# Three blocks of one expert moved ahead of the block table, beside the last scatters

## The chip, the cores and the metric

The kernel runs on one core of a Trainium2 chip, as one program in one launch. Its time is the device time of that launch in microseconds (us), the median of several runs. The work is written out in program order for each engine: PE (matrix products), DVE (vector), ACT (activations), POOL (GpSimd), and SP, which issues most of the DMAs. An engine carries out its own list in order and waits for the others by semaphores. [...]

## The reference

```python
X = np.fft.fft(np.fft.fft(x, axis=1), axis=2).real          # x: 8 x 3072 x 256
t = X.reshape(24576, 256)
logits = t @ w_gate                                          # 8 experts
e = np.argmax(logits, axis=1); gate = softmax(logits)[e]
y[e == k] = gate * (np.maximum(t @ w1[k], 0) @ w2[k])        # w1: 256 x 1024, w2: 1024 x 256
h = y @ w_in                                                 # 256 x 2048, w_in and w_out in float64
g = (a0 + a1 h + a2 h^2 + a3 h^3) / (1 + |b0||h| + |b1| h^2 + 1e-6)
out = g @ w_out                                              # 2048 x 256
```

## The kernel before, in words

**Phase 1** computes the Fourier transform, gate and sorting in 16 steps (`NS`), two for each of the 8 batch rows. A step has four first products (`stage1`, L438, PSUM pool psA), three groups of second products (`second`, L459 and L461), whose result y goes to SBUF through ACT and DVE (L465, L468; seven buffers), the squared norms on ACT (L496), the gate on DVE (`gate_a`, from L477), ranks within the expert on PE (`gate_rank`, L504 to L509, PSUM pool psS with one buffer), and positions, running counts `run` and gate values on DVE (`gate_b`, L519 to L537). Then POOL scatters 128 token rows at a time with an indirect DMA (L549) into `xs` in HBM, which has a region of R = 24832 rows for each expert. A row holds 256 numbers, the token's number and its gate. The gate of step s is finished in step s + 2 (`finish`), that of the last two steps in parts.

Beside that, each step takes one of 16 jobs: a weight matrix of one expert (`w1` or `w2`) is loaded, its norm summed (`job_sum`, L594, a product with a column of ones into `pa`, also in psS), scaled by a power of two, split into two f16 parts and stored in `ws` in HBM.

**The tail** (L834 to L931) follows the sixteenth step: the rest of the gate, the last twelve scatters, zero rows behind the last token of every expert (`c_z`, L855, each address a register that SP reads from `runi`), the block table on DVE (L865 to L931), and `partition_all_reduce` on POOL (L916) for the row scale `sx`. The table gives for each of the 103 blocks (`NSB`) of 256 rows the expert's weight rows (`widx`), the row in `xs` and the place in `ys` (`offi`), and a factor `rj`.

**Start-up.** A block j of an expert is four pieces: `m1a(j, 0)` and `m1a(j, 1)` (24 matmuls each, then hhi on ACT, L1136, and hlo on DVE, L1137) and `m1b(j, 0)` and `m1b(j, 1)` (24 each, then yw on ACT and DVE, the store to `ys`, and the token numbers to `idd`). Before it, `load(j)` brings its rows (`xr`, L1070), `pairs` splits them into f16 halves (xp; L1091 on ACT and L1092 on DVE for the first two blocks, POOL behind that), `transp` turns them on PE (L1105) and DVE copies them (xt, L1106). Weights come to `wslot[j % 2]`, for the first two blocks by SP (`gather_first`, L1320), then by POOL (`gather`, L908). The first 36 pieces (blocks 0 to 8, `np_`) run with nothing but a generator beside them: `prologue`, which decodes the float64 words of `w_in` and `w_out` quarter by quarter on DVE (`decode`, L207 to L215), splits them and ends with the scalar `og` (L1063). It has 33 steps; the loop calls one after each piece but i = 30, and the rest at i = 32.

**Unit loop.** Then come 385 units of the rational part (`m2a` and so on; the first activation is at L1231) with one piece beside each unit, until the blocks are used up. Block j goes to `ys` for good, and unit groups read `ys` in order, eight blocks behind.

The lists' order is the order of the code; no planner moves anything. Of the code that the steps below touch, the loop of the start-up and the zero rows:

```python
ins_z = [nc.sync.dma_start(out=xs[E * R:E * R + TB, :], in_=cst["c_z"])]
for e in range(E):
    v = nc.sync.value_load(runi[0:1, e:e + 1], min_val=e * R, max_val=e * R + NT)
    ins_z.append(nc.sync.dma_start(out=xs[ds(v, TB), :], in_=cst["c_z"]))
...
for i in range(np_):
    if i == 4 * LAG:
        step(100)
        bound_rows(0)
    piece(i, True)
    if i != 4 * LAG - 2:
        step(1)
```

Of the kernel before, what the change touches and what calls it, by code (L numbers as in the profile page):

```python
# [20 lines left out]
P = 128  # L21
# [8 lines left out]
DX = D + 2  # L30
R = 8 * S + TB
# [97 lines left out]
def fourier_moe_rational_kernel(ctx, tc, xl, wg, w1, w2, w_in, w_out, av, bv, cst, out):  # L129
# [48 lines left out]

    def pow2floor(dst, src):
# [9 lines left out]
    mq_in = keep.tile([P, 4], F32, name="mq_in")  # L189
    TINY = float(np.array([897 << 20], np.int32).view(np.float32)[0])  # L190
# [12 lines left out]
    def decode(r, dst, mx):  # L203
# [11 lines left out]
        V.tensor_reduce(out=mx, in_=dst, axis=AX.X, op=ALU.max, apply_absolute_value=True)  # L215

# [3 lines left out]
    with ExitStack() as c1:  # L220
# [24 lines left out]
        rc, onesf = carve(0, 137), carve(0, P)  # L245
        rs = cp.tile([P, 2, 137], F32, name="rs")
        fb = carve(0, 64).rearrange("p (i s b) -> p i s b", i=4, s=2)
        ids = carve(0, 24).rearrange("p (h t) -> p h t", h=2)
        msk, bigm = carve(0, 13), carve(0, 13)
        upto = carve(0, E * E).rearrange("p (a b) -> p a b", b=E)  # L250
# [340 lines left out]
        def job_sum(n):  # L591

            pa = psS.tile([P, 512], F32, tag="ss", name="pa")
# [87 lines left out]

        def edge_prep():
# [28 lines left out]
        nc.sync.dma_start(out=upto.rearrange("p a b -> p (a b)"), in_=cst["c_up"])  # L711
# [4 lines left out]
        for s in range(NS + 1):  # L716
# [4 lines left out]
            if on:  # L721
# [4 lines left out]
                if s > 1:  # L726
                    column_row(b, jh, u)
                stage1(b, jh, eo, 0, u)
# [88 lines left out]
            if s == NS - 1:  # L817
                gate_rank((p, 1), 4)
# [16 lines left out]
        p = NS - 1  # L835
        for q in range(2):
            load_words(q, raw_in[q])
# [3 lines left out]
        part_gate(p, 1)  # L841
        gate_rank((p, 1), 4)
# [3 lines left out]
        top_norm(*nq)  # L846
        *last, nq = part(p, 1)
        top_norm(*nq)
        V.tensor_copy(out=runi, in_=run)

# [8 lines left out]

        nbi = keep.tile([P, E], I32, name="nbi")
        nb = keep.tile([P, E], F32, name="nb")
        ctok = keep.tile([P, E], F32, name="ctok")
        V.tensor_tensor(out=nbi, in0=run, in1=ebase, op=ALU.subtract)  # L865
        V.tensor_scalar(out=nbi, in0=nbi, scalar1=8, scalar2=None, op0=ALU.logical_shift_right)
        V.tensor_copy(out=nb, in_=nbi)
# [564 lines left out]
```

## Time and profile before

| | us |
|---|---|
| median of 3 runs | 3607.03 (3605.4 to 3608.28) |
| profiled execution, device time | 3599.72 |
| its span, first to last instruction | 3597.9 |
| PE busy | 3460.9 (96%) |
| ACT busy | 3182.4 (88%) |
| DVE busy | 3049.6 (85%) |
| POOL busy | 2952.4 (82%) |
| mean granted clock of PE | 0.985 |

Times in the rows are microseconds from the start of the span, of one execution. A busy time is the sum over an engine's instructions; matmuls are pipelined, so theirs overlap a little. In brackets behind a row stands how long the engine was idle before it and what ended that. `SPq` and `POOLq` are the queues of SP and POOL themselves (issuing, waiting, reading registers). L12 is line 12 of the kernel.

### The profile page before, as it was taken

To read this page: it belongs to the slowest core of one execution; us is meant where nothing else is said; L and a number is where in the kernel's file an instruction comes from. 1 tells how busy PE (TensorE), PEld (TensorE's weight loads), DVE (VectorE), ACT (ScalarE), POOL (GpSimd) and SP (SyncE) were. 2 spreads that over 40 slices of the span, in tenths; PEclk is the share of its full clock that TensorE was granted. 3 is DMA by queue.
4 is the path that set the end of the run, shared out by engine and by line. 5 is a ranking of instruction groups with operands and counts; after the bars stand their busy time and mean duration, and the time that the engine had idled before them with its cause. 6 is when DMAs were issued, how large, how long until landed. Compare 5 with 4: busy or idle time off the path is not lost.

```text
span 3597.9 us, 75912 instructions
## 1 busy us (share of the span) xinstructions
PE 3460.9 (96%) x29948; PEld 2992.3 (83%) x29948; DVE 3049.6 (85%) x3483; ACT 3182.4 (88%) x4117; POOL 2952.4 (82%) x2840
## 2 busy tenths in 40 slices
PE   7998489999999999999999999999999999999997
PEld 4665378888888888888888888888888888888886
DVE  7886678888888888888888888888888888888887
ACT  5777349999999999999999999999999999999997
POOL 1666458888888888888888888888888888888887
PEclk9999699999999999999999999999999999999999
DMA  7675543321151112411151115121331113311110
GB/s 295 242 250 192 187 93 60 69 45 39 45 87 44 44 45 47 83 41 45 43 91 39 44 42 89 45 42 42 67 66 42 46 44 67 63 43 42 45 34 19
DMA packets 343974, 270.39 MB, mean 75 GB/s; under 512 B 181406, under 2 KB 318758, under 8 KB 336304
## 3 DMA queue, kind: packets, MB, share of 16 engines
q1 hardware_dynamic: 310528, 185.57, 20.7%
q0 software_dynamic: 33088, 79.97, 9.0%
q8 instruction: 234, 3.83, 0.6%
q14 instruction: 124, 1.02, 0.1%
HBM read 329.27 MB, written 96.92 MB: 118 GB/s over the span
## 4 chain that ended last, share of the span: by engine, by line
POOL 39%; ACT 29%; issue 14%; PE 7%; DVE 6%; DMA 3%; another core or an unknown queue 1%; SPq 0%; POOLq 0%; DVEq 0%; ACTq 0%
POOL glo L1265 12%; POOL bnd L1188 5%; POOL out_dram L1290 5%; ACT ghi L1264 5%; ACT hhi L1136 5%; POOL wslot L908 3%; ACT h L1249 3%; ACT L L1247 3%; POOL xr L1087 2%; PE po L1277 2%; PE h L1116 1%; PE h L1119 1%; PE h L1117 1%; POOL xp L1088 1%; DMA xs<-y,sli 1%
## 5 line engine op out<-in xcount | busy, mean ns | idle before, releaser
L1116 PE MATMUL h<-yr,win 128*128 128x256 f16 x3072 | 754.0, 273 | 3.1 <-DVE u__48174 L1252 1.7
L1117 PE MATMUL h<-yr,win 128*128 128x256 f16 x3072 | 753.9, 273 | 0.0
L1277 PE MATMUL po<-wout,ghi 128*128 128x256 f16 x6144 | 734.5, 273 | 8.5 <-POOL ghi L1262 7.0
L1277 PEld LDWEIGHTS <-ghi 128*128 128x128 f16 x6144 | 601.0, 98 | 80.2 <-POOL ghi L1262 8.3
L1119 PE MATMUL h<-yr,win 128*128 128x256 f16 x3072 | 586.4, 273 | 0.0
L1249 ACT ACTIVATE h<-L,bnd 128x1024 f32<-128x1024 f32 x385 | 429.7, 1116 | 35.9 <-DVE u__48728 L1240 0.7
L1116 PE MATMUL h<-xt,wslot 128*128 128x256 f16 x1648 | 405.8, 273 | 13.7 <-DVE hlo L1137 7.0
L1117 PE MATMUL h<-xt,wslot 128*128 128x256 f16 x1648 | 405.9, 273 | 0.0
L1277 PE MATMUL po<-wout,glo 128*128 128x256 f16 x3072 | 399.2, 273 | 1.4 <-POOL glo L1265 1.4
L1117 PEld LDWEIGHTS <-wslot 128*128 128x128 f16 x3296 | 323.1, 98 | 68.0 <-issue 31.5
L1116 PE MATMUL py<-hhi,wslot 128*128 128x256 f16 x1648 | 373.7, 274 | 4.3 <-ACT hhi L1136 2.9
L1117 PE MATMUL py<-hhi,wslot 128*128 128x256 f16 x1648 | 373.6, 274 | 0.0
L1116 PEld LDWEIGHTS <-wslot 128*128 128x128 f16 x3296 | 323.4, 98 | 47.4 <-issue 5.2
L1119 PEld LDWEIGHTS <-wslot 128*128 128x128 f16 x3296 | 323.8, 98 | 42.9 <-issue 4.3
L549 POOL DMA_INDIRECT xs<-y,sli x192 | 209.1, 1089 | 166.5 <-ACT sq L496 97.3
L1277 PEld LDWEIGHTS <-glo 128*128 128x128 bf16 x3072 | 300.4, 98 | 38.0 <-POOL glo L1265 3.1
L1116 PEld LDWEIGHTS <-win 128*128 128x128 f16 x3072 | 300.6, 98 | 36.6 <-DVE u__48174 L1252 1.9
L1117 PEld LDWEIGHTS <-win 128*128 128x128 f16 x3072 | 300.6, 98 | 36.6 <-issue 1.8
L1119 PEld LDWEIGHTS <-win 128*128 128x128 f16 x3072 | 300.6, 98 | 34.8
L1119 PE MATMUL h<-xt,wslot 128*128 128x256 f16 x1648 | 315.9, 273 | 0.0
L1137 DVE SCALAR_TENSOR_TENSOR hlo<-h,hhi 128x1024 f16<-128x1024 f32 x206 | 250.8, 1218 | 8.2 <-ACT hhi L1136 8.2
L1290 POOL DMA_INDIRECT out_dram<-o,id x192 | 199.2, 1038 | 49.5 <-issue 43.8
(4904 smaller groups left out, 9381.3 us busy)
## 6 DMA issues: line engine op xcount, KB each, us to landing
xr<-xs SPq DMA_DIRECT2D x103, 258.0 KB
ys<-yw SPq DMA_DIRECT2D x103, 256.0 KB
yr<-ys SPq DMA_DIRECT2D x96, 256.0 KB
xh<-x_l SPq DMA_DIRECT2D x14, 1536.0 KB
wf<-in_moe_w_dram SPq DMA_DIRECT2D x16, 1024.0 KB
ws<-wh SPq DMA_DIRECT2D x16, 1024.0 KB
wslot<-ws SPq DMA_DIRECT2D x4, 1024.0 KB
xh<-x_l SPq DMA_DIRECT2D x4, 768.0 KB
```

Of the source, the lines that this page charges most:

```text
L549: ins = nc.gpsimd.indirect_dma_start(out=xs, out_offset=bass.IndirectOffsetOnAxis(ap=sli[:, t0 + t:t0 + t + 1], axis=0), in_=y[:, t], in_o ...
L1116: nc.tensor.matmul(ps, lhsT=wa[i], rhs=xa[i], start=i == 0, stop=False)
L1117: nc.tensor.matmul(ps, lhsT=wb[i], rhs=xa[i], start=False, stop=False)
L1119: nc.tensor.matmul(ps, lhsT=wa[i], rhs=xb[i], start=False, stop=i == n - 1)
L1136: nc.scalar.activation(out=hhi[:, sl], in_=ps, func=AF.Relu)
L1137: V.scalar_tensor_tensor(out=hlo[:, sl], in0=ps, scalar=0.0, in1=hhi[:, sl], op0=ALU.max, op1=ALU.subtract)
L1188: nc.gpsimd.tensor_scalar(out=out, in0=in0, scalar1=a, scalar2=b, op0=op0, op1=op1)
L1249: nc.scalar.activation(out=ps, in_=L, func=AF.Exp, scale=-1.0, bias=st["bnd", j][3])
L1264: nc.scalar.activation(out=ghi, in_=w_, func=AF.Copy)
L1265: (V if fs[0] else nc.gpsimd).tensor_tensor(out=glo, in0=w_, in1=ghi, op=ALU.subtract)
L1277: nc.tensor.matmul(ps[:, q], lhsT=g[:, f - fs[0], q * P:(q + 1) * P], rhs=wout[:, h, 4 * u + f], start=g is ghi and u == 0 and f == 0 and ...
L1290: ins = nc.gpsimd.indirect_dma_start(out=out, out_offset=bass.IndirectOffsetOnAxis(ap=t[:, q:q + 1], axis=0), in_=o[:, q], in_offset=None, ...
```

## The change

At s = 14, when the tokens of steps 0 to 12 have been counted and their scatters are queued on POOL, the new `fullest` picks the expert that has most rows so far, on DVE, and has POOL reduce the largest norm until then over the partitions. In the last step, `early_rows` loads the first three blocks (K = 3, 768 rows) of that expert from `xs`, and `early_weights` its two weight halves to `wslot[0]`. `early_scale` gives them a row scale `sxe` of their own. In the tail these blocks 0 to 2 are computed: pairs, transposes, m1a and m1b stand between the operations of the gate, the scatters and the block table, which becomes a generator in two parts. What m1b gives is only copied from PSUM to `yf`; it is scaled by `ex1` and stored (`rows_out`) in the start-up. The table counts three blocks fewer for that expert and starts its places behind them. SP now issues the weight loads of block 3 ahead of the zero rows, the loads of blocks 3 to 5 behind them. The start-up loop runs from piece 12 to 35, with two prologue steps at i = 15, 18, 21, 24 and 27; `bound_rows(0)` comes ahead of the remaining steps. `pa` of `job_sum` moves from psS to psA. Constants that lay in `wslot[0]` get tiles of their own, because early weights now go there; `upto` is loaded later. `np_` and the unit loop stay as they are.

```diff
+K = 3
...
+        def fullest():
+            cnt, best = [gp.tile([P, E], F32, tag="cnt", name="cnt") for _ in range(2)]
+            V.tensor_tensor(out=cnt, in0=run, in1=ebase, op=ALU.subtract)
+            V.tensor_reduce(out=ex1, in_=cnt, axis=AX.X, op=ALU.max)
...
+            V.tensor_reduce(out=ex1, in_=nrm, axis=AX.X, op=ALU.max)
+            nc.gpsimd.partition_all_reduce(ex2, ex1, P, bass.bass_isa.ReduceOp.max)
+        def early_rows():
+            v = nc.sync.value_load(epos[0:1, 0:1], min_val=0, max_val=(E - 1) * R)
+            for k in range(K):
+                t = xe[k]
+                nc.sync.dma_start(out=t, in_=xs[ds(v + k * TB, TB), :].rearrange("(t p) c -> p t c", p=P))
...
+        def early_weights(h):
+            v = nc.sync.value_load(epos[0:1, 1:2], min_val=0, max_val=(E - 1) * P)
+            c = slice(4096 * h, 4096 * h + 4096)
+            nc.sync.dma_start(out=wslot[0][:, c], in_=ws[ds(v, P), c])
...
         def job_sum(n):
-            pa = psS.tile([P, 512], F32, tag="ss", name="pa")
+            pa = psA.tile([P, 512], F32, tag="s1", name="pa")
...
+                if s == NS - 1:
+                    early_rows()
                 stage1(b, jh, eo, 0, u)
...
                 send(*finish(s - 2))
+                if s == NS - 2:
+                    fullest()
             for n in old:
                 job_rest(n, 3)
                 job_store(n)
+            if s == NS - 1:
+                early_weights(0)
...
             if s == NS - 1:
+                early_weights(1)
+                early_scale()
...
+        for k in range(K):
+            st["x", k] = xe[k]
+            nc.sync.dma_start(out=idd[k * TB:(k + 1) * TB, :].rearrange("(t p) c -> p (t c)", p=P),
+                              in_=xe[k][:, :, D].bitcast(I32))
         for q in range(2):
-            load_words(q, raw_in[q])
+            pairs(0, q)
+        transp(0)
+        m1a(0, 0, True)
         gate_rank((p, 0), 8)
         second_norm(p, 2)
         ys_, sli, nq = part(p, 0)
         part_gate(p, 1)
+        m1a(0, 1, True)
         gate_rank((p, 1), 4)
         scatter(ys_[0], sli, 0)
         scatter(ys_[1][:, 0:2], sli, 4)
         rest = ys_[1][:, 2:4], sli, 6
         top_norm(*nq)
+        for q in range(2):
+            pairs(1, q)
+        m1b(0, 0, True)
+        transp(1)
         *last, nq = part(p, 1)
         top_norm(*nq)
         V.tensor_copy(out=runi, in_=run)
+        scatter(*rest)
+        send(*last)
+        V.tensor_reduce(out=nx1, in_=nrm, axis=AX.X, op=ALU.max)
+        nc.gpsimd.partition_all_reduce(nx2, nx1, P, bass.bass_isa.ReduceOp.max)
+        m1b(0, 1, True)
+        table = block_table()
+        m1a(1, 0, True)
+        for q in range(2):
+            pairs(2, q)
+        m1a(1, 1, True)
+        transp(2)
+        next(table)
+        for h in range(2):
+            gather_first(K, h)
         ins_z = [nc.sync.dma_start(out=xs[E * R:E * R + TB, :], in_=cst["c_z"])]
...
+        m1b(1, 0, True)
+        m1b(1, 1, True)
+        m1a(2, 0, True)
+        m1a(2, 1, True)
+        next(table)
+        m1b(2, 0, True)
+        m1b(2, 1, True)
...
+    load(K)
+    load(K + 1)
+    load(K + 2)
...
+    row_scale()
+    for q in range(2):
+        pairs(K, q)
...
-    for i in range(np_):
+    for i in range(4 * K, np_):
...
         if i == 4 * LAG:
+            bound_rows(0)
             step(100)
-            bound_rows(0)
         piece(i, True)
+        if i < 5 * K:
+            k = (i - 4 * K - 1) % K
+            rows_out(k, yf[k], ex1)
+            if k == K - 1:
+                load_words(1, raw_in[1])
         if i != 4 * LAG - 2:
-            step(1)
+            step(2 if i > 4 * K and i % 3 == 0 else 1)
```

In the diff, blank lines within functions are left out. Inside the early blocks, `pairs` uses ACT and DVE, `m1a` takes its PSUM from psB, `m1b` and the transposes from psA.

## Rows read from the trace of the kernel before

**Rows 1.** The page: span and instructions.

```profile
span 3597.9 us, 75912 instructions
```

**Rows 2.** Busy time by stretches; columns: us long, busy per engine, clock, DMA.

```profile
390.00:400.00 10.00, 0.38 (x8) 0.29 (x8) 7.40 (x39) 1.84 (x8) 5.12 (x6) 0.50 0.24 79
...
429.26:532.54 103.28, 91.82 (x850) 80.91 (x848) 86.49 (x115) 45.74 (x60) 54.82 (x62) 0.98 0.47 109
475.00:510.00 35.00, 29.81 (x267) 25.77 (x266) 33.34 (x33) 14.18 (x17) 20.82 (x20) 0.95 0.44 99
565.00:605.00 40.00, 39.58 (x363) 35.13 (x362) 34.52 (x33) 38.14 (x45) 33.55 (x34) 1.00 0.13 34
```

**Rows 3.** Timeline from og to the first unit: start, us, engine, line.

```profile
532.38 0.16 DVE L1063 RECIPROCAL og<-og 128x1 f32<-128x1 f32 x1
...
543.57 1.12 ACT L1231 ACTIVATE ab__5815<-h,coef 128x1024 f32<-128x1024 f32 x1 [0.62 <-PE pm L1176]
```

**Rows 4.** Waits of PE up to 360 us: total, times, longest.

```profile
PE pa L594 <- DVE run L521: 9.9, 6, 2.6
...
PE pa L594 <- ACT u L405: 4.9, 5, 1.5
```

**Rows 5.** Timeline of ACT, 359 to 368; in brackets the idle time before.

```profile
363.75 0.60 ACT L465 ACTIVATE y<-pq 128x516 f32<-128x516 f32 x1 [6.33 <-remote]
```

**Rows 6.** Timeline of POOL, 335 to 386: first and last scatter of step 13.

```profile
346.57 0.97 POOL L549 DMA_INDIRECT xs<-y,sli  x1 [4.98 <-issue]
...
360.65 0.98 POOL L549 DMA_INDIRECT xs<-y,sli  x1 [0.30 <-issue]
```

**Rows 7.** Timeline, 380 to 400: norms, exponential, runi.

```profile
389.40 0.42 ACT L496 ACTIVATE sq<-y 128x256 bf16<-128x256 f32 x1
...
391.44 0.24 ACT L516 ACTIVATE sh<-sh 128x64 f32<-128x64 f32 x1
...
396.42 0.16 DVE L849 CAST runi<-run 128x8 int32<-128x8 f32 x1
```

**Rows 8.** Timeline, 400 to 432: table, zero rows, first block, first decode.

```profile
400.23 0.17 DVE L887 CAST widx<-oj 128x2 int32<-128x2 f32 x1
...
400.74 12.35 SPq L855 DMA_DIRECT2D xs<-c_z  x6
...
416.00 0.43 SPq L1070 DMA_DIRECT2D xr<-xs  x1
...
417.25 0.35 SPq L1320 DMA_DIRECT2D wslot<-ws  x1
...
419.10 0.91 ACT L1091 ACTIVATE xp<-xr,gs 128x256 f16<-128x256 f32 x2 [2.03 <-DVE gs L1080]
...
421.12 0.69 DVE L1106 COPY xt<-pt 128x1024 f16<-128x1024 f16 x1 [0.60 <-PE pt L1105]
...
422.71 0.40 PE L1116 MATMUL h<-xt,wslot 128*128 128x256 f16 x1 [1.62 <-DMA wslot<-ws]
...
428.12 1.23 DVE L1137 SCALAR_TENSOR_TENSOR hlo<-h,hhi 128x1024 f16<-128x1024 f32 x1 [3.07 <-ACT hhi L1136]
...
429.26 0.68 DVE L207 TENSOR_SCALAR xh<-xh 128x1024 int32<-128x1024 int32 x1
```

**Rows 9.** Timeline, 281 to 283: one wait of line 594.

```profile
281.26 0.48 ACT L402 ACTIVATE u<-ps 127x384 f32<-127x384 f32 x1
...
281.74 0.17 DVE L521 TENSOR_TENSOR run<-pr,run 128x8 f32<-128x8 f32 x1
...
282.05 0.35 PE L594 MATMUL pa<-part,wslot 128*128 128x1 f32 x2 [2.21 <-DVE run L521]
```

**Rows 10.** Instructions of line 916 (durations in ns, first and last start).

```profile
L916 POOLq MODIFY_POOL_CONFIG  x2: 53/56/58, 409.9 to 410.0; - x2
L916 POOL PARTITION_ALL_REDUCE nx<-nx x1: 378/378/378, 416.0 to 416.0; - x1
```

**Rows 11.** Instructions of line 1080, the next of POOL after the reduction.

```profile
L1080 POOLq MODIFY_POOL_CONFIG  x2: 83/83/83, 416.4 to 416.4; - x2
```

More of the change, by code (lines that the diff above doesn't have):

```diff
@@ L189, in fourier_moe_rational_kernel @@
     mq_in = keep.tile([P, 4], F32, name="mq_in")
+    xe = [xw[0][:, 1024 + 516 * k:1540 + 516 * k].rearrange("p (t c) -> p t c", t=2) for k in range(K)]
     TINY = float(np.array([897 << 20], np.int32).view(np.float32)[0])
@@ new lines, in three, with m1a @@
+    def three(ps, wa, wb, xa, xb):
+        n = len(wa)
+        for i in range(n):
+            nc.tensor.matmul(ps, lhsT=wa[i], rhs=xa[i], start=i == 0, stop=False)
+            nc.tensor.matmul(ps, lhsT=wb[i], rhs=xa[i], start=False, stop=False)
+        for i in range(n):
+            nc.tensor.matmul(ps, lhsT=wa[i], rhs=xb[i], start=False, stop=i == n - 1)
+    def m1a(j, h, first):
+        W = wslot[j % 2 if j >= K else 0]
+        xhi, xlo = st["xs", j]
+        if h == 0:
+            st["h", j] = pl["h"]()
+        hhi, hlo = st["h", j]
+        ps = pl["h1"](first)
+        for f in range(4):
+            fo = (4 * h + f) * P
+            three(ps[:, f], [W[:, kc * F1 + fo:kc * F1 + fo + P] for kc in range(2)],
+                  [W[:, 2048 + kc * F1 + fo:2048 + kc * F1 + fo + P] for kc in range(2)],
+                  [xhi[:, kc] for kc in range(2)], [xlo[:, kc] for kc in range(2)])
+        sl = slice(4 * h, 4 * h + 4)
+        nc.scalar.activation(out=hhi[:, sl], in_=ps, func=AF.Relu)
+        V.scalar_tensor_tensor(out=hlo[:, sl], in0=ps, scalar=0.0, in1=hhi[:, sl], op0=ALU.max, op1=ALU.subtract)
@@ new lines, in m1b @@
+    def m1b(j, d, first):
+        W = wslot[j % 2 if j >= K else 0]
+        hhi, hlo = st["h", j]
+        if d == 0:
+            st["py", j] = pl["py"](first)
+        ps = st["py", j]
+        o = [4096 + f * D + d * P for f in range(8)]
+        three(ps[:, d], [W[:, i:i + P] for i in o], [W[:, 2048 + i:2048 + i + P] for i in o],
+              [hhi[:, f] for f in range(8)], [hlo[:, f] for f in range(8)])
+        if d == 1 and j < K:
+            nc.scalar.activation(out=yf[j], in_=ps, func=AF.Copy)
+        elif d == 1:
+            rows_out(j, ps, rj[:, j - K:j - K + 1])
@@ new lines, in fourier_moe_rational_kernel, with early_gs @@
+        V.tensor_copy(out=ident16, in_=ident)
+        gss = iter(range(K))
+        def early_gs():
+            k = next(gss)
+            return wide[:, 64 + 2 * k:66 + 2 * k]
+        pl.update(
+            id=ident16, gs=early_gs, xp=lambda: early("oo0", "xp"), xt=lambda: early("oo1", "xt"),
+            pt=lambda: psA.tile([P, 2, 2, TB], F16, tag="s1", name="pt"), h=early_h,
+            h1=lambda first: psB.tile([P, 4, TB], F32, tag="s2", name="h1"),
+            py=lambda first: psA.tile([P, 2, TB], F32, tag="s1", name="py"))
@@ L903, in fourier_moe_rational_kernel @@
-        V.tensor_scalar(out=move, in0=nb, scalar1=-float(TB), scalar2=float(R), op0=ALU.mult, op1=ALU.add)
-        places(0, E * R)
-        def gather(j):
-            i = j % 2
-            nc.gpsimd.indirect_dma_start(
-                out=wslot[i], out_offset=None, in_=ws,
-                in_offset=bass.IndirectOffsetOnAxis(ap=widx[:, j:j + 1], axis=0),
-                bounds_check=E * P - 1, oob_is_err=False)
-        scatter(*rest)
-        send(*last)
-        V.tensor_reduce(out=nx1, in_=nrm, axis=AX.X, op=ALU.max)
@@ L1335, in step @@
             next(side, None)
[L1337 to L1341 removed]
+    transp(K)
+    gather(K + 1)
+    pairs(K + 1, 0)
     NB = NT // TB
```

335 lines of the change are left out of this document (179 added, 156 removed).

## The prediction

> **What bounds the kernel now.** I read the page first: the span is 3597.9 us [rows 1] in a run of 3599.72, so 1.82 us lie outside the span; the median of the runs shown is 3607.03. The differences below are worked out on the profiled run and added to the median.
>
> Then the busy time by stretches. In the steady part PE has 39.58 of 40.00 us, DVE 34.52 [rows 2]. The change leaves the matmuls there alone: twelve pieces fewer before the unit loop, and the units take the rest as before. So the time moves by as much as the first unit moves; before, its first activation starts at 543.57 [rows 3], and the question is what comes ahead of that.
>
> Ahead of it lie three stages. In phase 1, PE waits in front of line 594 [rows 4]; towards its end it is the scatters: ACT's line 465 sits 6.33 us, up to 363.75, for a release that the view calls remote [rows 5], and what ends just before is POOL's last scatter of step 13, issued at 360.65 [rows 6]; y has seven buffers, which the scatters free. In the tail, 390 to 416, PE is almost idle (0.38 of the first 10 us, DVE 7.40 [rows 2]) while DVE does gate and block table, with runi at 396.42 [rows 7], and SP writes zero rows up to the load at 416.00 [rows 8]. In the start-up, 429 to 533, PE has 91.82 of 103.28 us and DVE 86.49: a mixed bound, and where the decoding lies densest (475 to 510) it is DVE, at 33.34 of 35.00 [rows 2]. The change takes PE work out of the start-up and puts it into the tail, where PE is free. What it doesn't take along is DVE's decoding.
>
> **Phase 1.** `pa` leaves the PSUM pool psS for psA. At 282.05 PE waits for `run` (DVE, 281.74 + 0.17 = 281.91), which frees psS; the ACT evacuation that frees psA ended at 281.26 + 0.48 = 281.74 [rows 9]. That is 0.2 to 0.3 us to win; over eleven waits -3 us. Bounds: nothing, and both rows of waits whole, 9.9 + 4.9 = 14.8 us [rows 4]; I take the three rows of one wait.
>
> `fullest` at s = 14 is eleven small DVE operations like runi (0.16 [rows 7]), 1.8 us, and DVE waits a good deal there: nothing, 1.8 without that cover. Its partition_all_reduce, though, goes into POOL's queue between the scatters of step 12 and those of step 13. For the reduction of the kernel before, two MODIFY_POOL_CONFIG stand at 409.9 to 410.0 and the reduction starts at 416.0: 6.1 us, then 0.38 [rows 10]; and behind it there are two more at 416.4 [rows 11]. Between the two groups of scatters POOL idled 4.98 us, up to 346.57 [rows 6]. Into that now go 6.1 + 0.4, so the next scatter is 1.5 us late, 1.8 with the semaphores around it. Whether the way back costs 6.1 as well, no row says, since POOL had nothing due then. Bounds +1.8 and +7.9; the nearest row is that of the same instruction on the way out, so +7.9. As the scatters free y, and y holds up ACT, this passes to the tail in full.
>
> [...]
>
> `early_rows` reads xs, so on SP it waits for the landing of step 12's scatters, and the scatters of step 13 wait for it: three loads of the kind that goes out at 416.00 and is in xt by 421.81 [rows 8]; they lie inside POOL's own delay, so nothing on top, 1 us if the swap back is free. `early_weights` waits for the stores of ws; behind it on SP stand raw words and zero rows, not due until the table is done: hidden, and the weights have until the first matmul at 392; come late, they would show as PE waiting for wslot there.
> Phase 1: -3 + 7.9 = **+4.9** (-2.5, or -13 with all of line 594's waits, to +7.9).
>
> **The tail, on the old time axis.** The three blocks now stand in program order between the gate's operations on ACT, DVE and PE, and the table's first result, widx, comes only after most of them.
> 1. ACT is free for xp at 389.40, ahead of the last four norms [rows 7]. From xp's start (419.10) to xt's end (421.81) 2.7 us [rows 8]: 392.1.
> 2. First matmul to the start of hlo 5.41, to its end 6.64 (422.71, 428.12 + 1.23) [rows 8]; it ran at the half clock in part, and PE comes from idleness here too (granted clock 0.50 at 390 to 400 [rows 2]). So hlo starts at 397.5, and the four norms, 2.0 together (389.40 to 391.44 [rows 7]), end on ACT at 399.6.
> 3. From the exponential (391.44) to runi's end (396.58) it was 5.1 us [rows 7]; between them now stand on DVE a second hlo, xt, and two lo halves of xp at some 0.9: 1.23 + 0.69 + 1.8 = 3.7 [rows 8]. So runi is done at 408.4, 12 us later.
> 4. Ahead of the table stand m1b(0,1), m1a(1,0) and m1a(1,1): PE from 405.6, three times 24 matmuls at 91.82/850 = 0.108 us [rows 2] = 7.8, to 413.4; then hhi (1.1, as the activation of the same size [rows 3]), hlo and xt, to 416.4. From runi to widx 396.42 to 400.40 [rows 7, 8], with one more operation 4.1: widx at 420.5 instead of 400.4.
> 5. SP: two weight loads at 1.25 us (416.00 to 417.25 [rows 8]) and the first zero row: 424. From runi's end to the load of xr it was 416.00 - 396.58 = 19.4 us of zero rows [rows 7, 8], and the load waits for the last one to land. 424 + 19.4 = 443.4 instead of 416.00: **+27.4**.
> Bounds of it: the zero rows at a pitch of 1.25 instead of 12.35/6 = 2.06 [rows 8] give 6.5 back, a first block at the full clock 1.7; four more pieces at the half clock, 4 x 24 x 0.108, cost 10.4. So +19 to +38.
>
> The second reduction, the rest of the table, m1b(1), m1a(2) and m1b(2) lie beside the zero rows: PE is done at about 436. Upto, ident16 and the constants that move are ready long before: nothing. The three idd stores have 30 us before anything waits for them.
>
> **The start-up.** From load to first decode 13.26 us before (416.00 to 429.26) [rows 8]; the weights are now there, for which PE waited 1.62, but a `rows_out` comes ahead: unchanged. From there to the end of `og` it was 532.54 - 429.26 = 103.28 us [rows 3, 8]. DVE loses the hlo and xt of three blocks, 6 x 1.23 + 3 x 0.69 = 9.4 [rows 8]: 86.49 - 9.4 = 77.1 us. It is now the bound, since PE loses twelve pieces, 12 x 2.6 = 31 of its 91.82 [rows 2]. The prologue's 33 steps all still follow the first decode: 24 of them within the pieces 12 to 31, nine at i = 32, where there were two. Taken at the share of the stretch that DVE bounds, 33.34/35.00 = 95% [rows 2]: 81 us. Bounds: 77 at 100%, 92 at the 84% of the whole. **-22.3** (-26 to -11). From og to the first unit the same pieces follow, 543.57 - 532.54 = 11.0 [rows 3]; bound_rows, one small operation ahead instead of behind, is 0.1.
>
> **Sum:** 4.9 + 27.4 - 22.3 = +10.0, so 3617 us; with its own bounds from 3609 to 3625.
>
> **Rivals.**
> - *The swap's way back or the zero rows are cheap* (not slower). The scatters don't wait for the way back, -6.1: 3610.9; or the zero rows' pitch falls to the 1.25 of the loads behind them, since no scatters run beside them any more, -6.5: 3610.5; both: 3604. For it: no row shows a wait for the way back. Against: the same instruction took 6.1, and the zero rows need a register load each in both kernels. It decides from 3 us off the sum.
> - *Phase 1 gives back all that line 594 waits* (faster). 14.8 instead of 3, -11.8; and as PE then leads the scatters, POOL's idle time grows by at least the 6.1 of the way back: 3617 - 17.9 = 3599. For it: the waits are real. Against: psA has users of its own, and is free only 0.2 earlier. It decides when most of the eleven waits vanish with nothing in their place.
> - *The tail runs at the half clock* (slower). Four more pieces before widx at twice the time, +10.4: 3627. For it: 0.50 from 390 to 400. Against: matmuls that began at 422.71 had PE at 0.98 over the stretch from 429 [rows 2].
> - *The start-up becomes bound by the blocks, not by DVE*: 24 of 36 pieces in two thirds of 103 us would be 69 us, under DVE's 77: it can't be.
>
> **How the numbers follow.** What a measurement here can tell from no change is about 0.2%, 7.2 us: slower is over 3614.2, faster under 3599.8. Chances: forecast 0.46 (0.05 of it under 3614), half clock 0.14, first rival 0.26, line 594 0.14. So slower 0.55, same 0.31, faster 0.14. The range leaves out about a tenth on each side, 3599 to 3629.
>
> **What would show it.** Two pairs of MODIFY_POOL_CONFIG in phase 1, and the first scatter of step 13 eight us later than before against the rest of its step (else the way back is free); line 594's waits down by 3 or by 12; the first xr load at about 448, 32 us later; the zero rows' pitch near 2.1; DVE at 95% from about 461 to 542, with PE near 75%; a longer stretch at i = 32 in which PE stands; the first unit at about 553, the units unchanged. I am wrong if the load of xr comes before 440, or if DVE has idle time in the start-up.

## The result and the profile after

The changed kernel is slower. In runs side by side its median is 3630.28 us (3623.71 to 3633.47) against 3607.66 us: a ratio of 1.0064 [1.0050, 1.0077], +22.6 us, where +10 had been forecast. The direction was right, the size was not, and the time lies 1.3 us outside the range. The profiled run of the changed kernel took 3623.71 us.

The page, first lines:

```profile
span 3621.9 us, 75904 instructions
...
PE 3469.2 (96%) x29948; PEld 2994.6 (83%) x29948; DVE 3054.9 (84%) x3511; ACT 3184.4 (88%) x4126; POOL 2936.0 (81%) x2825
```

The span is 24.0 us longer than in [rows 1], and the first unit starts 26.24 us later (569.81, the last row below, against 543.57 in [rows 3]): all of the loss lies ahead of the unit loop, as the prediction had it.

Timeline of DVE, from `runi` to `widx`, and the end of `og`:

```profile
411.38 0.17 DVE L1113 CAST runi<-run 128x8 int32<-128x8 f32 x1
...
421.35 1.22 DVE L312 SCALAR_TENSOR_TENSOR early_h<-h,early_h 128x1024 f16<-128x1024 f32 x1 [9.68 <-ACT early_h L311]
...
430.86 0.17 DVE L1026 CAST widx<-oj 128x2 int32<-128x2 f32 x1
...
466.79 0.69 DVE L217 TENSOR_SCALAR xh<-xh 128x1024 int32<-128x1024 int32 x1
...
561.47 0.17 DVE L1284 RECIPROCAL og<-og 128x1 f32<-128x1 f32 x1
```

Timeline of SP, from the weights of block 3 to the first row load:

```profile
431.80 1.60 SPq L241 DMA_DIRECT2D wslot<-ws  x2
433.44 0.62 SPq L1130 DMA_DIRECT2D xs<-c_z  x1
434.86 9.73 SPq L1133 DMA_DIRECT2D xs<-c_z  x8
452.94 1.61 SPq L1289 DMA_DIRECT2D xr<-xs  x2
```

Timeline of ACT, the first unit:

```profile
569.81 1.11 ACT L1377 ACTIVATE ab__5796<-h,coef 128x1024 f32<-128x1024 f32 x1 [0.62 <-PE pm L1322]
```

From these rows and [rows 3, 7, 8] comes the table, stage by stage: how much later (+) each mark is than before. The second pair are the same two kernels in other runs, where both are some 33 us faster (before 3574.65, changed 3597.31, ratio 1.0062); without it the two causes below can't be told apart. Its two traces, `before_again` and `after_again`, were taken on different chips. Of the experiments, `no_sync`, `no_par`, `before_pa` and `before_decode` ran beside a kernel before of some 3600 us, as the first pair did (the first group); all others ran beside one of 3575 to 3579 us (the second group).

| mark | forecast | this pair | second pair |
|---|---|---|---|
| `runi` done | +16.7 | +15.0 | +15.7 |
| `widx` done | +25.0 | +30.6 | +24.1 |
| first `xr` load | +32.3 | +36.9 | +33.1 |
| first decode | +32.3 | +37.5 | +31.4 |
| `og` done | +10.0 | +29.1 | +22.5 |
| first unit | +10.0 | +26.2 | +20.8 |

The times of the second pair, before and changed: `runi` 375.06 and 390.75, `widx` 378.90 and 403.03, load 391.81 and 424.87, decode 406.65 and 438.06, `og` 510.02 and 532.47, first unit 519.89 and 540.65.

In the second pair every mark up to the first decode is within 1.0 us of its forecast; then 13.4 us are missing at once. That the marks fit so closely is partly luck: in the twelve traces of the second group in which the kernel is the changed one up to there, `runi` is done anywhere from 390.75 to 395.50, and this is the earliest of them. The length from `runi` to `widx` is steady (12.3 to 12.4 us in those of them in which that part is unaltered). In this pair it is 19.5, so 7.4 us more are lost there.

Busy time of the changed kernel in the tail and from the first decode to `og` (columns as in [rows 2]):

```profile
390.00:400.00 10.00, 8.64 (x72) 6.55 (x72) 3.83 (x10) 3.71 (x12) 0.00 (x0) 0.73 0.01 2
...
431.03:452.94 21.91, 9.42 (x85) 8.05 (x83) 13.59 (x36) 3.05 (x5) 1.08 (x1) 0.78 0.81 301
466.79:561.64 94.85, 67.27 (x547) 55.43 (x545) 77.69 (x105) 38.19 (x53) 36.82 (x37) 0.86 0.41 109
```

The last row is the heart of the case. DVE works 77.69 us, as forecast (77.1), but the stretch lasts 94.85 us, not 81: DVE is idle for 17.2 us. Before, it was idle for 103.28 - 86.49 = 16.8 us [rows 2]. **The stretch became shorter by the DVE work that was taken out (8.8 us of work, 8.4 us of time), and the sum of DVE's idle time stayed.** PE lost 24.6 us of work there, and DVE's idle time is no shorter for it.

What DVE waits for in that stretch (total, times, longest), before (from 429.40, so without the hlo that ends there):

```profile
DVE hlo L1137 <- ACT hhi L1136: 5.2, 6, 1.7
DVE yw L1153 <- ACT yw L1150: 3.8, 3, 2.7
DVE yw L1153 <- DMA idd<-xr: 3.3, 1, 3.3
```

and after:

```profile
DVE yw L1297 <- ACT yw L1294: 8.9, 3, 4.7
DVE hlo L312 <- ACT hhi L311: 3.4, 3, 2.0
DVE wout L1230 <- ACT wout L1229: 1.4, 2, 1.2
```

and what PE waits for there:

```profile
PE pr L1211 <- DVE mq_out L1208: 10.2, 1, 10.2
PE py L292 <- ACT hhi L311: 7.6, 3, 5.2
PE py L295 <- DVE hlo L312: 6.5, 3, 3.4
PE pr L1211 <- DVE mq_in L1208: 2.6, 1, 2.6
```

The waits for hlo did fall with the number of pieces (5.2 to 3.4 us), but those for yw rose (3.8 + 3.3 to 8.9): equal idle time before and after is the sum of the two, not a fixed price.

DVE and PE stand in turn: DVE at yw and hlo until PE and ACT have done a piece, PE at the maximum of the words (`pr`) and at hlo until DVE has done its part. Each engine's list is in order, and such a wait is not filled with later work of its own (in the 5.30 us of the row below DVE works 0.30, with prologue steps still to come); it takes another order of the list to do that (`late_rows` below takes 6.6 us off the wait for yw). The longest wait shows the turn. PE stands idle for 2.6 us until DVE's maximum lets `pr` go at 500.47. Only then does the m1b behind it start; its output, yw, is next in DVE's list, and DVE waits 4.73 us for it, up to 505.78. PE in that time:

```profile
500.50:505.80 5.30, 5.30 (x32) 3.95 (x33) 0.30 (x2) 0.71 (x2) 0.50 (x1) 0.68 0.47 92
```

From 501.27 to 504.95 the matmuls stand 0.21 us apart instead of 0.11 (granted clock 0.68 over the row); at 0.11, by an estimate from these two, the piece would end 1.8 us earlier.

### The profile page after: what moved, and what is told of

Its sections match the earlier page's. It is cut to its first block, busy times and chain, and to the rows that moved or that the text cites. A ratio compares the mean times of both kernels' runs of the same rounds, so it can differ in the third digit from the quotient of the medians.

```text
span 3621.9 us, 75904 instructions
## 1 busy us (share of the span) xinstructions
PE 3469.2 (96%) x29948; PEld 2994.6 (83%) x29948; DVE 3054.9 (84%) x3511; ACT 3184.4 (88%) x4126; POOL 2936.0 (81%) x2825
## 3 DMA queue, kind: packets, MB, share of 16 engines
q1 hardware_dynamic: 310528, 185.57, 20.8%
## 4 chain that ended last, share of the span: by engine, by line
POOL 26%; PE 26%; ACT 20%; DVE 15%; issue 11%; DMA 1%; another core or an unknown queue 1%; SPq 0%; POOLq 0%; ACTq 0%; DVEq 0%
POOL glo L1411 8%; PE po L1423 6%; POOL out_dram L1436 4%; ACT ghi L1410 4%; PE ps L549 4%; PE h L292 3%; PE h L295 3%; PE h L293 3%; ACT h L1395 3%; ACT hhi L311 3%; DVE h L1397 2%; POOL wslot L232 2%; POOL bnd L1334 2%; ACT L L1393 2%; POOL xr L263 2%
## 5 line engine op out<-in xcount | busy, mean ns | idle before, releaser
L295 PE MATMUL h<-yr,win 128*128 128x256 f16 x3072 | 586.4, 273 | 0.0
L292 PE MATMUL h<-xt,wslot 128*128 128x256 f16 x1600 | 395.5, 274 | 11.0 <-DVE hlo L312 6.6
L293 PE MATMUL h<-xt,wslot 128*128 128x256 f16 x1600 | 395.6, 274 | 0.0
L292 PE MATMUL py<-hhi,wslot 128*128 128x256 f16 x1600 | 364.0, 274 | 9.0 <-ACT hhi L311 7.6
L295 PEld LDWEIGHTS <-wslot 128*128 128x128 f16 x3296 | 324.8, 99 | 51.4 <-issue 11.6
L293 PE MATMUL py<-hhi,wslot 128*128 128x256 f16 x1600 | 364.0, 274 | 0.0
L295 PEld LDWEIGHTS <-win 128*128 128x128 f16 x3072 | 300.6, 98 | 34.7
L295 PE MATMUL h<-xt,wslot 128*128 128x256 f16 x1600 | 307.7, 274 | 0.0
L312 DVE SCALAR_TENSOR_TENSOR hlo<-h,hhi 128x1024 f16<-128x1024 f32 x200 | 243.4, 1218 | 9.7 <-ACT hhi L311 9.7
```

Source lines behind the costliest of these rows:

```text
L292: nc.tensor.matmul(ps, lhsT=wa[i], rhs=xa[i], start=i == 0, stop=False)
L293: nc.tensor.matmul(ps, lhsT=wb[i], rhs=xa[i], start=False, stop=False)
L295: nc.tensor.matmul(ps, lhsT=wa[i], rhs=xb[i], start=False, stop=i == n - 1)
L312: V.scalar_tensor_tensor(out=hlo[:, sl], in0=ps, scalar=0.0, in1=hhi[:, sl], op0=ALU.max, op1=ALU.subtract)
```

## The experiments

Ratios are to runs of the kernel before on the same chip, with their 95% intervals. "Start-up" is the time from the first decode to the end of `og`.

**The same pair again** (the second pair). The changed kernel, unaltered (`after_again`):

> The changed kernel itself, once more, for a second trace and as the measure of the runs beside it. Theory A (PE's stream is held up beside the scatters at fixed work): its first m1a of block 1 takes some 11 us again, 410 to 420, and the kernel stands 22 to 26 us over the kernel before. Theory B (these gaps are chance of one execution): the gaps lie elsewhere or are gone, and the block table is some 8 us earlier in this trace.

3597.31 us, 1.0062 [1.0048, 1.0075], 22.7 us over the kernel before; the gaps are gone, as in theory B, and `widx` comes 12.3 us behind `runi`. But they are no chance of one execution either: in `no_sync` and `no_par`, of the first group, they are back (19.8 and 19.5 us from `runi` to `widx`). The kernel before, unaltered (`before_again`):

> The kernel before itself, for a trace on the same chip as the runs beside it. Its first decode to og takes 103 us again and og to the first unit 11 us; what differs between chips lies ahead of that, in phase 1 and the tail (by 10 to 25 us).

3575.93 us; from `og` to the first unit it is 9.9 us, not 11. Windows of the start-up, kernel before:

```profile
406.65:510.02 103.37, 90.51 (x851) 80.12 (x849) 86.68 (x115) 45.77 (x60) 56.66 (x64) 1.00 0.48 105
```

and the changed kernel:

```profile
438.06:532.47 94.41, 66.67 (x547) 54.96 (x544) 77.58 (x105) 38.25 (x53) 36.86 (x37) 0.87 0.42 109
```

DVE's idle time is 16.7 and 16.8 us: the finding repeats.

**Half of DVE's maximum** (`half_reduce`; the maximum of each decoded quarter over half its columns):

```diff
-V.tensor_reduce(out=mx, in_=dst, ...)
+V.tensor_reduce(out=mx, in_=dst[:, 0:512], ...)
```

> The changed kernel; the search for the largest weight (line 225) looks only at the first half of the columns of each quarter, so that 8 operations of DVE fall from 1.22 to 0.6 us, 4.9 us of work less in the start-up. Theory A (DVE is the bound of the start-up): first decode to og falls from 94.8 to about 90. Theory B (DVE and PE wait for each other in turn, and the order of the steps sets the time): it falls by less than 3.

3593.27 us, 1.0041 [1.0027, 1.0054]. Windows of the start-up:

```profile
442.08:532.08 90.00, 65.48 (x547) 54.51 (x545) 73.84 (x105) 38.45 (x53) 35.77 (x37) 0.87 0.44 115
```

DVE works 3.7 us less and the stretch is 4.4 us shorter: DVE's work is on the path although DVE is idle for 18% of the stretch.

**No maximum over the partitions** (`no_sync`; each partition scales by its own maximum, so both trips to PE in `split_scale` are left out):

```diff
-pr = psM.tile(...); nc.tensor.transpose(pr[0:1, :], mq[:, 0:1], ident)
...
-V.tensor_scalar(out=sc, in0=pb, ...)
+V.tensor_scalar(out=sc, in0=mq[:, 0:1], ...)
```

> The changed kernel without the maximum over the partitions in the two split scales: each partition takes its own, so that DVE's reduction no longer goes through PE's transpose and product (lines 1211 and 1215) and back. Theory B (PE, which waits in its queue for DVE's last reduction, comes late with the m1b behind it, at the half clock, and DVE then waits 4.7 us for that m1b): DVE's waits for yw fall from 8.5 us to under 4, first decode to og from 94.4 to 86 to 90. Theory A (the idle time comes from DVE and PE handing blocks to each other all along, the two transposes add no more than their own 2 us): 91 to 94.

3621.25 us, 1.0054 [1.0041, 1.0067]. Windows of the start-up:

```profile
475.52:564.57 89.05, 62.67 (x536) 52.99 (x533) 76.74 (x103) 38.19 (x53) 38.97 (x37) 0.89 0.47 116
```

5.8 us shorter than 94.85, with only 0.95 us less work on DVE: the trips to PE cost the path 5 us of waiting. The wait for yw falls from 8.9 to 6.0, not under 4 as theory B had it; the waits for the trips themselves (1.5) go, and 0.5 of those for hlo.

**Both at once** (`half_nosync`):

> The changed kernel without the two maxima over the partitions and with the maximum of each decoded quarter over half its columns (so with other scales of the weights). Alone, these gave 5.8 us (94.85 to 89.05, on one chip) and 4.4 us (94.4 to 90.0, on the other). Theory A (both lie in one chain, DVE's work and the trips to PE in turn): they add, 94.4 - 5.8 - 4.4 = 84 us from the first decode to og. Theory B (the pieces of the blocks, with their loads and stores, set a pace of their own just below): 88 to 90 us.

3588.88 us, 1.0028 [1.0016, 1.0039]. Windows:

```profile
442.35:527.30 84.95, 61.61 (x536) 52.57 (x533) 72.75 (x103) 38.25 (x53) 39.16 (x37) 0.90 0.48 122
```

84.95 against 84 expected of one chain: the two reliefs add, and no pace of the blocks at 88 to 90 stands in between.

**A lighter decoding** (`light_decode`; the multiplication that zeroes tiny numbers is left out, the maximum taken over 64 columns):

```diff
-V.scalar_tensor_tensor(out=dst, in0=hi, scalar=TINY, in1=dst, op0=ALU.is_ge, op1=ALU.mult)
-V.tensor_reduce(out=mx, in_=dst, ...)
+V.tensor_reduce(out=mx, in_=dst[:, 0:64], ...)
```

> The changed kernel without the last multiplication of the decoding (the one that puts tiny numbers to zero) and with the maximum over 64 of 1024 columns: about 2.35 us less on DVE in each of eight quarters, 18.8 us. Theory A (nine tenths of what DVE loses come out, as 4.4 of 4.9 did): 94.4 - 17 = 77 us from the first decode to og. Theory B (the blocks' own pace lies not far below): 84 us or more, with DVE under 75% busy.

3582.88 us, 1.0019 [1.0009, 1.0028]. Windows:

```profile
439.62:518.64 79.02, 64.89 (x545) 54.32 (x543) 59.26 (x97) 38.44 (x53) 35.67 (x37) 0.89 0.50 131
```

18.3 us less work, 15.4 us less time, 2 us short of the 77 expected: DVE's idle time has grown to 19.8 (of it 10.0 at yw, 4.6 at hlo). That the pace of the blocks begins to be felt there is a reading, not tried. The pieces are all in these 79 us, so the forecast's 81 was within their reach; it was DVE's chain that did not allow it.

**Order alone.** `sched` spreads the prologue steps otherwise over the pieces (`step((1, 2, 2, 1)[i % 4])` behind every piece, also at i = 30):

> The changed kernel with another order of the prologue's steps: 1, 2, 2, 1 behind the four pieces of every block, 30 of the 33 done before i = 32 instead of 24. Theory B (in the changed kernel DVE sits idle 15 us in the start-up because yw waits for an m1b which waits for the hlo of just before, with only one or two steps between them, and PE sits through the nine steps at i = 32): first decode to og falls from 95 to 80 to 85, and the kernel is 8 to 14 us faster than the changed one. Theory A (DVE's work alone, any order will do): 93 to 96, no change.

3597.17 us, 1.0048 [1.0035, 1.0062]; start-up 93.8. DVE's wait for yw falls to 6.6 us, but 3.8 us of waiting for raw words come in its place. `late_rows` puts the output of a block behind the prologue step that follows:

```diff
+elif d == 1 and first:
+    later.append((j, ps, rj[:, j - K:j - K + 1]))
...
 step(2 if i > 4 * K and i % 3 == 0 else 1)
+while later:
+    rows_out(*later.pop())
```

> The changed kernel, with the output of each start-up block (yw on ACT and DVE, and its stores) put behind the prologue step that follows its last piece. On the chip where the changed kernel took 94.4 us from the first decode to og, DVE spent 8.5 us of that waiting for ACT's half of yw. Theory A (DVE and PE take turns: DVE stands in its list at yw until PE and ACT are done with the piece, PE then stands at the next sync): that wait goes, 86 to 90 us, first unit 4 to 8 us earlier. Theory B (the wait is slack that another order only moves): 92 to 95 us, no change.

3597.71 us, 1.0053 [1.0036, 1.0070]; start-up 91.6. DVE's waits in it:

```profile
DVE hlo L313 <- ACT hhi L312: 4.2, 3, 2.4
DVE mxs L1219 <- PE pb L1218: 3.3, 2, 2.6
DVE yw L1300 <- ACT yw L1297: 1.9, 2, 1.4
```

In the unaltered kernel (`after_again`):

```profile
DVE yw L1297 <- ACT yw L1294: 8.5, 2, 4.6
DVE hlo L312 <- ACT hhi L311: 3.4, 3, 2.0
...
DVE mxs L1216 <- PE pb L1215: 0.7, 1, 0.7
```

Of 6.6 us that the yw wait loses, 3.4 turn up at hlo and at `pb`, and the start-up gains 2.8: between the two expectations. `decode_early` decodes the first quarter ahead of the first piece of the start-up (its second quarter overwrites one early block's output before it is stored):

> The changed kernel with the decoding of the first quarter of w_in on DVE ahead of block 3's pairs, where DVE waited 9.8 us for the rows of block 3; the prologue then has two steps less. If this work alone counts (theory A): the first hlo of block 3 stays where it is and og comes 5 to 6 us earlier. Theory B: og comes 5 to 8 us earlier too, since the nine steps at i = 32 become seven; the start-up is then some 89 us from the first hlo of block 3. If nothing is gained, the first quarter was not on the path.

3594.64 us, 1.0044 [1.0030, 1.0057], no gain beyond the spread. In its trace (3599.85, the slowest of its five runs) `og` comes 109.1 us behind the load of xr, in the unaltered kernel 107.6: neither theory's 5 us is there. `lump_late` runs the remaining prologue steps ahead of piece 34 instead of 32:

> The changed kernel, with the remaining prologue steps run ahead of piece 34 instead of piece 32, and one step each behind pieces 32 and 33. At i = 32 PE stood about 10 us beside DVE's remaining steps. Theory A (DVE is the bound, so og ends where it did; the two pieces, 5 us of PE, now lie beside it instead of behind): og 0 to 3 us later, first unit 3 to 5 us earlier. Theory B (what stands between og and the first unit is the first row load yr and the bound's own chain, not the pieces): first unit within 1 us.

3596.02 us, 1.0051 [1.0034, 1.0068]. First decode to first unit takes 99.3 us instead of 102.6, as expected of DVE as the bound: two pieces of PE now lie beside it. In the medians this is not clear of the spread.

**The tail.** `zero_first` puts the zero rows right behind `runi`, `table_first` puts the table and the weights of block 3 ahead of the early m1b(0,1) and m1a(1), `zero_table` does both:

> The changed kernel with the zero rows issued right behind runi, as the kernel before has them, and the weight loads of block 3 behind them. Theory A (the load of block 3 waits for zero rows that start only at 433): zero rows go out from 412, land by 432, the load goes out some 2 us behind offi, at 437 instead of 453, the first decode at about 452 instead of 467, and the kernel is 13 to 16 us faster than the changed one. Rival (the first blocks wait for the 2 MB of weights anyway): the load is early, but PE's first matmul of block 3 is not before 455, and the gain is under 6 us.

> The changed kernel with the block table's first part, the weight loads and the zero rows straight behind runi, ahead of m1b(0,1), m1a(1,0) and m1a(1,1). Theory A (the early blocks stand ahead of the table and hold up everything behind): widx at 416 instead of 431, the load of block 3 at about 437, block 3's first matmul then waits for the early blocks, done at 445; first decode at about 456, 8 to 14 us faster than the changed kernel. Rival (the early blocks lose as much as the table gains, since they now wait for DVE): first decode stays near 465 and the gain is under 4 us.

> Both edits: zero rows behind runi, then the table ahead of the early blocks 1 and 2. Theory A: the load of block 3 at about 432; from there it is the early blocks' own chain on PE, ACT and DVE that block 3 waits for, so first decode at about 452, no more than 3 us better than the zero rows alone: 14 to 18 us faster than the changed kernel. Rival (the two add up): 22 to 28 us faster than the changed kernel, that is level with the kernel before.

3591.82 us, 1.0039 [1.0026, 1.0053]; 3595.86 us, 1.0055 [1.0041, 1.0069]; 3596.99 us, 1.0058 [1.0044, 1.0071]. Phase 1 ends at other times in these traces, so their marks are taken from the end of `runi`. In `zero_first` xr is loaded 16.7 us earlier than in `after_again` (17.4 us behind `runi` instead of 34.1), as theory A had it, but the first decode is only 8.3 us earlier (39.0 instead of 47.3); the median is 5.5 us lower. What ACT waits for between 405 and 424 in it:

```profile
ACT xh L325 <- PE py L295: 5.3, 1, 5.3
ACT xh L325 <- DMA xr<-xs: 4.6, 1, 4.6
ACT nx L1184 <- DVE nx L1188: 3.8, 1, 3.8
```

ACT's first step of the row scale (L1184) waits for DVE, which is in the rest of the block table until 421.4; xp can only start behind it, at 423.06. So with the load out of the way the table is next. `table_first` has widx 8.2 us and the load 11.1 us earlier behind `runi` and decodes 3.0 us earlier; its median is within the spread of the unaltered kernel. `zero_table` is no better than that: its load waits 8.3 us for PE's early pieces (SPq L1289 <- PE h L295) and comes 23.0 us behind `runi`, so its two parts don't add.

**Phase 1.** `no_par` leaves out the early reduction over the partitions (the early scale then differs by partition); `before_pa` is the kernel before with `pa` in psA alone:

> The changed kernel without POOL's reduction over the partitions at s = 14; a copy on DVE stands for it, so the early blocks' row scale differs by partition. [...] By the forecast's figure (7.9) it would be 6 to 8 us faster. [...]

> The kernel before with one edit: pa of job_sum in psA instead of psS. Forecast's theory: line 594's waits fall by about 3 us, and the time by 2 to 4. Rival (all of line 594's waits go): 8 to 15 us faster. Rival (psA's buffers are then missing to stage1): no change or slower.

3627.89 us, 1.0075 [1.0063, 1.0088]; 3600.33 us, 0.9999 [0.9988, 1.0009]. Neither moves the time beyond the spread. In `before_pa` the running count of step 13 is 4.3 us earlier than before, but its first scatter only 0.3 us (346.26 against 346.57) and the first count of step 14 0.4 us (363.5 against 363.9): the scatters take the gain back. POOL in `no_par`, around the place where the reduction was:

```profile
336.99 0.97 POOL L660 DMA_INDIRECT xs<-y,sli  x1 [0.30 <-issue]
346.92 0.97 POOL L660 DMA_INDIRECT xs<-y,sli  x1 [8.96 <-DVE nq L655]
...
417.88 0.97 POOL L660 DMA_INDIRECT xs<-y,sli  x1 [0.30 <-issue]
424.89 0.38 POOL L1117 PARTITION_ALL_REDUCE nx<-nx  x1 [6.04 <-DVE wide L255]
```

and in the changed kernel:

```profile
337.86 0.97 POOL L660 DMA_INDIRECT xs<-y,sli  x1 [0.30 <-issue]
345.00 0.38 POOL L806 PARTITION_ALL_REDUCE ex<-ex  x1 [6.17 <-DMA xh<-xs]
348.08 1.20 POOL L660 DMA_INDIRECT xs<-y,sli  x1 [2.71 <-DVE nq L655]
...
415.62 0.97 POOL L660 DMA_INDIRECT xs<-y,sli  x1 [0.30 <-issue]
416.63 0.32 POOL L1117 PARTITION_ALL_REDUCE nx<-nx  x1
```

The scatter waits for the gate (nq) with and without the reduction. Behind the running count of its step the first scatter of step 13 stands 2.4 us in the kernel before and 6.4 us in the changed one, but 6.4 us also in `no_par` and in `before_pa`, which have no early reduction: in this group it adds nothing.

**Towards a better version.** `before_decode` is the kernel before with two quarters decoded beside the tail; `before_late` the kernel before with `late_rows` and `lump_late`; `combined` the changed kernel with `zero_first`, `late_rows` and `lump_late`:

> The kernel before with one edit: the decoding of the first two quarters of w_in on DVE ahead of the start-up, the first behind the block table (DVE idle there 5 us, up to the row scale), the second behind the first block's transposes (idle 6 us, up to the first hlo). If the start-up of the kernel before is bound by DVE in good part, as the forecast has it: og comes 7 to 11 us earlier, and the kernel is 6 to 10 us faster than the kernel before. If PE bounds it (91.8 of 103.3 us): the nine steps' work is hidden already, 0 to 3 us faster.

> The kernel before with the two moves of order in its start-up that helped the changed one: the output of a start-up block behind the prologue step, the remaining steps at piece 34 behind bound_rows(0). DVE there waited 9.5 us for ACT's half of yw and PE 5.1 us for the maximum of bound_rows. Theory A (DVE's waits are in its chain too): first unit 4 to 8 us earlier, ratio 0.998 to 0.999. Theory B (PE, at 90.5 of 103.4 us, bounds this start-up beside DVE, so the waits only move): within 2 us, ratio 0.9995 to 1.0005.

> The changed kernel with the zero rows ahead of the block table (alone 5.5 us under the changed kernel), the block outputs behind the prologue step (start-up 2.8 us shorter alone) and the remaining steps at piece 34 (first decode to first unit 3.3 us shorter alone). Theory A (the waits of DVE lie in one chain, so the gains add): 11 to 12 us under the changed kernel, still 8 to 11 us over the kernel before, ratio 1.002 to 1.003. Theory B (late outputs and late remaining steps take the same slack): 7 to 9 us under the changed kernel, ratio about 1.004.

3608.25 us, 1.0024 [1.0014, 1.0034]; 3582.53 us, 1.0014 [1.0005, 1.0023]; 3587.49 us, 1.0029 [1.0018, 1.0040]. In `before_decode` `og` ends 133.1 us behind `runi`, 2.9 us earlier than before (136.0), and the first unit starts 28 us behind `og`: PE is busy with the pieces until 539.4 and then waits 5.7 us for `yr`. So there `og` is not what the first unit waits for. In `before_late` PE waits between `og` and the first unit for this:

```profile
PE h L1116 <- DMA yr<-ys: 6.6, 1, 6.6
```

where in the kernel before it waited 5.1 us for `bound_rows`. The load of `yr` reads what the blocks stored in `ys`, so there the first unit hangs on block stores, not on DVE; that the later outputs made it late fits, but the two edits were not tried apart. `combined` is the best of the changed versions (by the ratio some 12 us better, as if the gains added; in its trace, though, first decode to first unit is 100.7 us, no better than the 99.8 and 99.3 of `late_rows` and `lump_late` alone, so that the sum is not shown), and still slower than the kernel before. No version beat it.

## Why the prediction was wrong

**The step that failed** is the start-up: "Taken at the share of the stretch that DVE bounds, 33.34/35.00 = 95% [rows 2]: 81 us." The measured stretch is 94.85 us (94.41 in the second pair), 13 to 14 us more, with DVE at 82%. DVE's work was right to 0.6 us. Wrong was that its idle time would go because PE has less to do. Work plus idle time gives each run: 77.6 + 16.8 (changed), 73.8 + 16.2 (`half_reduce`), 76.7 + 12.3 (`no_sync`), 72.8 + 12.2 (`half_nosync`), 77.8 + 13.8 (`late_rows`), 59.3 + 19.8 (`light_decode`). Less work shortens the work, fewer trips to PE or another order shortens the idle time; fewer pieces took 1.8 us off the waits for hlo and put as much on those for yw. The densest 35 us of decoding hold six hlo and two outputs, with 1.3 us of waiting, but neither of the two maxima over the partitions (464 to 468 and 512 to 519 before), and beside these stood most of DVE's waits: from 464 to 474 and from 512 to 528 some 13 of 16.8 us. So their share cannot be carried over the stretch. The prediction's own sign came true: "I am wrong if the load of xr comes before 440, or if DVE has idle time in the start-up." The prediction's upper bound of 92, from the share of the whole, was much nearer; the idle time of before as a fixed amount, 77.1 + 16.8 = 93.9, would have hit it, but by luck, as the two kinds of wait moved against each other. One thing that may hold the idle time up was seen but not tried by itself: PE, now with less to do, stands at those trips, and its granted clock over the stretch is 0.86 where it was 0.98 [rows 2], so the piece that DVE waits for is itself slower (1.8 us in the one above).

**Runi to widx** was right where PE ran through: 12.3 us in the second pair, 12.1 forecast. In the profiled run of the first it took 19.5. Timeline of PE there, in m1a(1, 0), where a matmul otherwise follows every 0.11 us:

```profile
411.47 0.27 PE L295 MATMUL h<-early,wslot 128*128 128x256 f16 x1 [0.71 <-issue]
412.88 0.27 PE L292 MATMUL h<-early,wslot 128*128 128x256 f16 x1 [1.14 <-issue]
...
415.06 0.27 PE L292 MATMUL h<-early,wslot 128*128 128x256 f16 x1 [1.80 <-issue]
416.47 0.37 PE L293 MATMUL h<-early,wslot 128*128 128x256 f16 x1 [1.14 <-issue]
417.88 0.37 PE L295 MATMUL h<-early,wslot 128*128 128x256 f16 x1 [1.04 <-issue]
```

Single matmuls stand 0.7 to 1.8 us apart with no wait that the profile names. With 0.35 us before the next one this is 6.2 us; behind it the granted clock is 0.50 from 418.6 to 422.6 (a matmul each 0.21 us instead of 0.11), some 1.9 us more. DVE's 9.68 us before `early_h` are this same time. In the second pair the same piece and m1a(1, 1) together run from 390.1 to 395.5 without a pause. So between runi and widx the tail at the half clock, a rival, was there for 4 us only, and behind the pauses. Ahead of runi it was there more (granted clock 0.73 from 390 to 400), but runi came 1.7 us earlier than forecast. One term of that part was too large: the two lo halves of xp were put at 0.9 us each on DVE, but the 0.91 of [rows 8] is for two (x2), on ACT; on DVE one takes 0.48.

**Widx to the load, load to first decode** were right in length: 21.9 us against 22.9, and 13.85 against 13.26. But the first was right by luck: zero rows did fall to a pitch of 9.73/8 = 1.2 us, the cheap end of the first rival, and the load came no earlier, because it waits for the last one to land (SPq L1289 <- DMA xs<-c_z, 7.0 us). From the end of the last issue to the load it was 416.00 - 413.09 = 2.9 us before [rows 8] and is 452.94 - 444.59 = 8.3 us now. The price per issue was 0.8 us too high, which over eight is 6.7 us, and the landing was 5.4 us too short. DMA moves 301 GB/s from 431 to 453, with its engines 81% busy: two weight halves (2.1 MB), nine times zero rows (2.4 MB) and, to make up the 6.6 MB of that row, POOL's load of the weights of block 4 (2.1 MB), which goes out at 440.97. Which of them makes the landing long was not tried; in `table_first`, where POOL's load goes out behind that of xr, it is at most 5.2 us. Nor was the price of an issue the change's doing alone: in `before_again` the pitch is 10.48/8 = 1.3 us, with scatters beside it.

**Phase 1**, +4.9 forecast, came out at +0.2 by the first running count of step 14 and +2.5 by the two that follow (+1.6 and +2.5 in the second pair). The 7.9 us for the swap were too high by more than 5: no run shows the 6.1 us in them for a way back ahead of the scatters, and no row of before could tell. Only one pair of MODIFY_POOL_CONFIG stands in phase 1 (339.1), so the scatters from 348.08 on start without a second one, and the second reduction, at 416.63, has none ahead of it and starts 0.04 us behind its scatter; the way back stands at 442.1 (L255). The way out took 339.1 to 345.0, 5.9 us. The profile puts that wait down to the landing of the early rows, but `no_par` parts the two: there the tail's reduction is the first one, the pair stands ahead of it (419.1), and it starts at 424.89, 5.8 us later, where the profile names DVE. So in these traces the 6 us go with the pair, whatever is named. Yet they cost no time that shows, since the scatter behind it waits longer, for the gate. `pa` lost most of line 594's waits (the 14.8 us of [rows 4] to nothing; all of that line's, 18.3 to 3.8), as a rival had it, and gained nothing, as `before_pa` shows: in their place PE waits 8.5 us (4.3 and 4.2) for ACT to free psA (`ps`, L438), the users of its own that the prediction held against that rival.

**Og to first unit** is 8.2 us instead of the 11.0 that were to stay: `bound_rows` ahead of the remaining steps takes away 5.1 us that PE waited for it, which the prediction had put at 0.1; 2.0 us of waiting for hlo stand in their place.

The differences of this pair, against the forecast: -1.7 up to runi, +7.4 to widx, -1.0 to the load, +0.6 to the first decode, +13.9 to og, -2.9 to the unit: +16.3, of 26.2 - 10.0.

## What to carry to other kernels

Split a stretch into an engine's work and its idle time, and ask of each part by itself what the change does to it, and of each wait which piece it is for: here 24.6 us of work taken from PE ended no more of DVE's waiting, as some waits shrank (hlo, 5.2 to 3.4 us) while others grew by as much (yw, 7.1 to 8.9). A share read from the densest part of a stretch (95% here) was a bound, not an estimate for the whole (82%). Where a transfer waits for stores ahead of it, count their landing: here the load came 8.3 us behind the end of the last issue instead of 2.9, so that issues at 1.2 us instead of the 2.06 forecast brought nothing, and an earlier place for them brought less than it freed (16.7 us at the load, 8.3 at the decode): look for the next thing due, here the table and the row scale.

## What was unexpected of the hardware

- In the changed kernel's trace one pair of MODIFY_POOL_CONFIG stands ahead of the first reduction over the partitions (339.1) and one behind the second (442.1), and none at the 36 scatters of y between them. Some 6 us stood between the pair and the reduction behind it (5.8 in `no_par`, 5.9 in the changed kernel, 6.1 before, 6.2 in `before_again`), under whatever name the profile gave the wait.
- PE's unexplained pauses of 0.7 to 1.8 us stood beside scatters at a pitch of 1.28 us and ended within 3 us of the last one (415.62). Up to 600 us they add up to 24.1 us in the profiled run of the changed kernel and 8.2 before, 14.6 in `no_sync`, 14.3 in `no_par`, 12.4 in `before_pa`, 8.1 in `before_decode`, but 0 to 0.4 in every run of the second group, whatever the kernel. What makes them was not tried and stays open.
